# Reading the moving operand of a product column by column from its two halves in turn

## The chip, the cores and the metric

The kernel runs on one core of a Trainium2 chip. The metric is the device time of one execution in microseconds (us). Engines are named as the profile names them: PE is TensorE's matmul, PEld its weight load, DVE is VectorE, ACT is ScalarE, POOL is GpSimd, SP is SyncE, which here issues nearly all DMAs.

## The reference

Eight sequences of 3008 tokens with 256 channels go through a Fourier mixing layer, and all 24064 tokens then through a feed-forward layer of width 2048:

```python
def _attn_ref(x, w_r, w_i, b_r, b_i):
    X = np.fft.rfft(x, axis=1)
    Xr, Xi = (X.real.astype(np.float32), X.imag.astype(np.float32))
    Yr = Xr @ w_r - Xi @ w_i + b_r
    Yi = Xr @ w_i + Xi @ w_r + b_i
    lam = 0.01
    Yr = np.sign(Yr) * np.maximum(np.abs(Yr) - lam, 0.0)
    Yi = np.sign(Yi) * np.maximum(np.abs(Yi) - lam, 0.0)
    Y = Yr.astype(np.float64) + 1j * Yi.astype(np.float64)
    return np.fft.irfft(Y, n=x.shape[1], axis=1).astype(np.float32)

def _moe_ref(x, w_in, w_out):
    h = np.maximum(x @ w_in, 0.0)
    return (h * h @ w_out).astype(np.float32)
```

All of it is float32. Every token is a column of its own in the feed-forward layer: no step of that layer mixes two tokens.

## The kernel before

The Fourier transform of a sequence is cut into factors 47 and 64; its steps are small products on TensorE, with trips through DRAM scratch between them (steps a, b, mix, c and d in the names of tiles). The transform of the next sequences and the feed-forward layer of the present one run side by side.

The feed-forward layer works on chunks of `CH = 512` tokens, 47 of them (8 x 3008 / 512). A chunk's input stands in SBUF as `xt`, two tiles [128, 2, 512] of type float32r: the high part and the low part of the number, each with the 256 channels as two blocks of 128 partitions (index k) and the 512 tokens contiguous along the row. A float32 product is made of three products of such parts (`mm3`, lines 183 to 188: high times high, high times low, low times high).

The main loop (line 1115) runs over rounds; a round is one chunk and one of `NU = 8` pairs of hidden blocks, so there are 47 x 8 = 376 rounds. In a round:

- `mm1` (line 971), the first product, makes two blocks (a = 0, 1) of 128 hidden units by 512 tokens, `ph` in PSUM. The stationary operand is a 128x128 block of `w_in` (`wi`), the moving operand is `xt`, 512 columns wide. For each a there are two channel blocks k and three part products: 12 matmuls of 512 columns. In the rounds called `halved` (130 of them) the last product of the second block is cut into two of 256 columns (lines 983 to 986).
- `squares` (line 991) on ACT takes `ph` out of PSUM with Relu (line 995) and squares it (line 996) into `g`; `sums` on DVE makes three more combinations of quarter blocks, so that `g` has seven slabs of 256 columns. A slab combines the two hidden blocks and the two 256-column halves of the chunk.
- three rounds later (`LAG = 3`) `mm2` (line 1018), the second product, multiplies the seven slabs (split into `gh` and `gl`) by seven combinations of `w_out` blocks: 21 matmuls of 256 columns (14 at line 1023, 7 at line 1027), summed over the eight rounds of a chunk in four banks `po`. `put_together` then makes the 256 output channels by 512 tokens of the chunk and stores them contiguously in `outT`.

Between the two products a round may also hold the transform's matmuls: `psb` (line 228), `psd` (line 277), `psa`, `psm`, `psc` (through `mm3`). The order on each engine is written out by hand: `manual_schedule` keeps the order of the program text, and a plan of places (`p1`, `p2`, `e`, `f`, ...) puts the transform's steps into the rounds. On the host, `token_order()` puts the columns of `outT` back into the order of tokens.

## Time and profile before

| | |
|---|---|
| time, median of 3 runs | 2524.14 us (2523.18 to 2525.43) |
| span of the profiled execution, first to last instruction | 2521.5 us |
| median time less that span | 2.6 us |
| PE busy | 2503.5 us (99%) |
| PEld busy | 2260.2 us (90%) |
| DVE busy | 2097.8 us (83%) |
| ACT busy | 1991.8 us (79%) |
| POOL busy | 17.0 us (1%) |
| DMA engines, main queue | 20.9% of 16 engines |

The profiled execution has only its span listed, not a time of its own; the median of the timed runs stands 2.6 us above it. Busy time is the union of an engine's records. The duration of a matmul in a row runs from its start to a modelled end, and successive matmuls overlap in it; the pace of a stream of matmuls is read from the difference of their starts. A window is given in us from the start of the span.

### The profile page before, as it was taken

To read this page: it belongs to the slowest core of one execution; us is meant where nothing else is said; L and a number is where in the kernel's file an instruction comes from. 1 tells how busy PE (TensorE), PEld (TensorE's weight loads), DVE (VectorE), ACT (ScalarE), POOL (GpSimd) and SP (SyncE) were. 2 spreads that over 40 slices of the span, in tenths; PEclk is the share of its full clock that TensorE was granted. 3 is DMA by queue.
4 is the path that set the end of the run, shared out by engine and by line. 5 is a ranking of instruction groups with operands and counts; after the bars stand their busy time and mean duration, and the time that the engine had idled before them with its cause. 6 is when DMAs were issued, how large, how long until landed. Compare 5 with 4: busy or idle time off the path is not lost.

```text
span 2521.5 us, 42247 instructions
## 1 busy us (share of the span) xinstructions
PE 2503.5 (99%) x16648; PEld 2260.2 (90%) x16648; DVE 2097.8 (83%) x3179; ACT 1991.8 (79%) x2776; POOL 17.0 (1%) x29
## 2 busy tenths in 40 slices
PE   9999999999999999999999999999999999999999
PEld 5689999999999999999999999999999999999998
DVE  5798888888888888888888888888887888777776
ACT  4788887888788887888878878788787788777776
POOL 0100000000000000000000000000000000000000
PEclk9999999999999999999999999999999999999999
DMA  8612222222121121212122121221111111101000
GB/s 266 207 55 66 74 88 68 65 76 73 54 75 60 50 70 57 71 50 67 60 69 63 54 70 50 70 62 61 58 56 56 38 54 48 39 21 34 17 25 18
DMA packets 110622, 164.66 MB, mean 65 GB/s; under 512 B 9513, under 2 KB 59673, under 8 KB 110234
## 3 DMA queue, kind: packets, MB, share of 16 engines
q1 hardware_dynamic: 110282, 161.85, 20.9%
q8 instruction: 132, 2.16, 0.4%
q14 instruction: 64, 0.52, 0.1%
q10 hardware_dynamic: 144, 0.13, 0.0%
HBM read 86.97 MB, written 74.97 MB: 64 GB/s over the span
## 4 chain that ended last, share of the span: by engine, by line
PE 88%; ACT 5%; DVE 4%; issue 1%; DMA 1%; SPq 0%; DVEq 0%; ACTq 0%
PE po L1023 21%; PE ph L187 11%; PE ph L188 11%; PE ph L186 11%; PE po L1027 11%; PE psd L277 3%; PE psb L228 3%; PE psm L186 3%; PE psm L188 3%; PE psm L187 3%; ACT g L995 1%; PE ph L986 1%; PE ph L983 1%; PE ph L984 1%; ACT g L996 1%
## 5 line engine op out<-in xcount | busy, mean ns | idle before, releaser
L1137 DVE TENSOR_TENSOR gl<-g,gh 128x1792 fp32r<-128x1792 f32 x376 | 759.5, 2020 | 22.4 <-ACT gh L1132 15.4
L995 ACT ACTIVATE g<-ph 128x512 f32<-128x512 f32 x752 | 408.2, 595 | 417.1 <-PE ph L188 297.4
L1023 PE MATMUL po<-gh,wo 128*128 128x256 f32 x5250 | 681.5, 280 | 3.1 <-DVE o L1053 2.1
L1132 ACT CAST gh<-g 128x1792 fp32r<-128x1792 f32 x376 | 637.2, 1695 | 3.5 <-PE po L1023 0.8
L1023 PEld LDWEIGHTS po<-gh,wo 128*128 128x128 f32 x5250 | 631.2, 188 | 6.5 <-DVE o L1053 5.9
L186 PE MATMUL ph<-xt,wi 128*128 128x512 f32 x1374 | 538.2, 392 | 2.2 <-ACT g L995 2.0
L188 PE MATMUL ph<-xt,wi 128*128 128x512 f32 x1374 | 537.4, 391 | 0.0
L187 PE MATMUL ph<-xt,wi 128*128 128x512 f32 x1374 | 537.3, 391 | 0.0
L1001 DVE TENSOR_TENSOR g<-g 128x512 f32<-128x512 f32 x376 | 259.3, 690 | 290.3 <-ACT g L996 288.4
L996 ACT ACTIVATE g<-g 128x1024 f32<-128x1024 f32 x376 | 399.5, 1062 | 12.0
L1027 PE MATMUL po<-gl,wo 128*128 128x256 f32 x2625 | 359.2, 276 | 0.0
L1027 PEld LDWEIGHTS po<-gl,wo 128*128 128x128 f32 x2625 | 325.7, 188 | 0.0
L188 PEld LDWEIGHTS ph<-xt,wi 128*128 128x128 f32 x1374 | 258.0, 188 | 55.9
L186 PEld LDWEIGHTS ph<-xt,wi 128*128 128x128 f32 x1374 | 257.9, 188 | 49.6 <-ACT g L995 2.8
L187 PEld LDWEIGHTS ph<-xt,wi 128*128 128x128 f32 x1374 | 258.0, 188 | 44.3
L1003 DVE TENSOR_TENSOR g<-g 128x256 f32<-128x256 f32 x376 | 159.9, 425 | 12.9
L1002 DVE TENSOR_TENSOR g<-g 128x256 f32<-128x256 f32 x376 | 159.8, 425 | 12.9
L186 PE MATMUL psm<-wm,xh 128*128 128x256 f32 (+1 forms) x552 | 159.7, 289 | 1.6 <-ACT x L232 1.3
L188 PE MATMUL psm<-wm,xl 128*128 128x256 f32 (+1 forms) x552 | 158.2, 287 | 0.0
L187 PE MATMUL psm<-wm,xh 128*128 128x256 f32 (+1 forms) x552 | 158.0, 286 | 0.0
L277 PEld LDWEIGHTS psd<-tD,din 120*128 120x128 f32 (+1 forms) x832 | 108.2, 191 | 9.7 <-issue 1.9
L228 PEld LDWEIGHTS psb<-tB,bin 128*128 128x128 f32 x768 | 99.8, 191 | 13.1 <-issue 3.7
(139 smaller groups left out, 2800.5 us busy)
## 6 DMA issues: line engine op xcount, KB each, us to landing
bin<-s SPq DMA_DIRECT2D x96, 256.0 KB
s<-evc SPq DMA_DIRECT2D x96, 256.0 KB
outT_dram<-o SPq DMA_DIRECT2D x92, 256.0 KB
din<-s SPq DMA_DIRECT2D x96, 240.0 KB
xin<-in_xp_dram SPq DMA_DIRECT2D x72, 240.0 KB
s<-eva SPq DMA_DIRECT2D x72, 240.0 KB
s<-eva SPq DMA_DIRECT2D x38, 192.0 KB
w<-in_moe_w_in_dram SPq DMA_DIRECT2D x8, 512.0 KB
```

Source lines behind the costliest of these rows:

```text
L186: nc.tensor.matmul(out, l0, r0, start=start, stop=False, **kw)
L187: nc.tensor.matmul(out, l0, r1, start=False, stop=False, **kw)
L188: nc.tensor.matmul(out, l1, r0, start=False, stop=stop, **kw)
L228: nc.tensor.matmul(ps[:, k, :, q, :], tv[:, q, k], tB[:, 0:r + 2:r + 1], start=True, stop=True)
L277: nc.tensor.matmul(ps[:, k, part], t[:n, s:s + P], tD[:n, tab + part, :n], start=True, stop=True)
L995: nc.scalar.activation(g[:, 2 * a:2 * a + 2], ph[a].rearrange("p (t m) -> p t m", t=2), AF.Relu)
L996: nc.scalar.activation(g[:, 0:4], g[:, 0:4], AF.Square)
L1001: nc.vector.tensor_sub(g[:, 4:6], g[:, 1:4:2], g[:, 0:2])
L1023: nc.tensor.matmul(out, wo_[k][j][:, s], gh[:, s], start=j == 0 and half == 0 and k == 0, stop=False, skip_group_check=True)
L1027: nc.tensor.matmul(out, wo_[0][j][:, s], gl[:, s], start=False, stop=j == NU - 1, skip_group_check=True)
L1132: nc.scalar.copy(split_[r - 1][0], hid[r - 1])
L1137: nc.vector.tensor_sub(gl, hid.pop(r - 1), gh.bitcast(F32))
```

## The change

`crossed` is a view of a tile's row of 512 columns in which column 0 of the first half comes first, then column 0 of the second half, then column 1 of the first, column 1 of the second, and so on: an access pattern of 256 steps of 4 bytes with 2 steps of 1024 bytes inside it. `mm1` hands its moving operand to the matmuls in this view. The tiles themselves, what is written to them, the number of instructions and their order on every engine stay as they were; the rows of the instruction order differ by their line numbers alone. Column j of `ph`, and of all that follows, then belongs to another token of the same chunk, and numpy puts the columns of `outT` back after the run (`places`).

```diff
+def crossed(x):
+    return x.rearrange("p (a i) -> p i a", a=2)
+
+def places(n):
+    return np.arange(n).reshape(2, n // 2).T.reshape(-1)
...
-                w, x = (wi_[0][:, k, fs], wi_[1][:, k, fs]), (xts[c][0][:, k], xts[c][1][:, k])
+                w, x = (wi_[0][:, k, fs], wi_[1][:, k, fs]), (crossed(xts[c][0][:, k]), crossed(xts[c][1][:, k]))
                 if halved and a and k:
                     nc.tensor.matmul(ph[a], w[0], x[0], start=False, stop=False)
                     nc.tensor.matmul(ph[a], w[0], x[1], start=False, stop=False)
                     for n in range(0, CH, HALF):
-                        nc.tensor.matmul(ph[a][:, n:n + HALF], w[1], x[0][:, n:n + HALF], start=False, stop=n > 0)
+                        nc.tensor.matmul(ph[a][:, n:n + HALF], w[1], x[0][:, n // 2:(n + HALF) // 2], start=False, stop=n > 0)
                 else:
                     mm3(ph[a], w, x, k == 0, k == 1)
...
-    got = got.reshape(D, nb, S)
+    chunks = np.empty((D, nb * S // CH, CH), got.dtype)
+    chunks[:, :, places(CH)] = got.reshape(D, -1, CH)
+    got = chunks.reshape(D, nb, S)
```

## Rows read from the trace of the kernel before

**Rows 1.** The page: span, busy time (share) xinstructions, PE and its granted clock in tenths.

```profile
span 2521.5 us, 42247 instructions
PE 2503.5 (99%) x16648; PEld 2260.2 (90%) x16648; DVE 2097.8 (83%) x3179; ACT 1991.8 (79%) x2776; POOL 17.0 (1%) x29
...
PE   9999999999999999999999999999999999999999
...
PEclk9999999999999999999999999999999999999999
```

**Rows 2.** The page: chain of work that ended last, shares by engine and line.

```profile
PE 88%; ACT 5%; DVE 4%; issue 1%; DMA 1%; SPq 0%; DVEq 0%; ACTq 0%
PE po L1023 21%; PE ph L187 11%; PE ph L188 11%; PE ph L186 11%; PE po L1027 11%; PE psd L277 3%; PE psb L228 3%; PE psm L186 3%; PE psm L188 3%; PE psm L187 3%; ACT g L995 1%; PE ph L986 1%; PE ph L983 1%; PE ph L984 1%; ACT g L996 1%
```

**Rows 3.** Groups on PE: line, out<-in, shapes, xcount | busy us, mean ns | idle before.

```profile
L186 PE MATMUL ph<-xt,wi 128*128 128x512 f32 x1374 | 538.2, 392 | 2.2 <-ACT g L995 2.0
...
L187 PE MATMUL ph<-xt,wi 128*128 128x512 f32 x1374 | 537.3, 391 | 0.0
...
L986 PE MATMUL ph<-xt,wi 128*128 128x256 f32 x260 | 51.5, 280 | 0.0
L983 PE MATMUL ph<-xt,wi 128*128 128x512 f32 x130 | 50.6, 389 | 0.0
L984 PE MATMUL ph<-xt,wi 128*128 128x512 f32 x130 | 50.6, 389 | 0.0
```

**Rows 4.** Timeline of PE in one round: start us, us, engine line op.

```profile
1211.26 0.39 PE L186 MATMUL ph<-xt,wi 128*128 128x512 f32 x1
1211.49 0.40 PE L187 MATMUL ph<-xt,wi 128*128 128x512 f32 x1
...
1214.00 0.28 PE L186 MATMUL psa<-fh,tAs 120*120 120x256 f32 x1
...
1214.71 1.76 PE L1023 MATMUL po<-gh,wo 128*128 128x256 f32 x14
1216.31 0.96 PE L1027 MATMUL po<-gl,wo 128*128 128x256 f32 x7
1217.10 0.28 PE L186 MATMUL psm<-wm,xh 128*128 128x256 f32 x1
```

**Rows 5.** What PE waited for in the whole span: us in total, times, longest.

```profile
PE psa L488 <- DMA x<-in_xu_dram: 2.3, 2, 1.2
PE po L1023 <- DVE o L1053: 2.1, 11, 0.3
PE ph L186 <- ACT g L995: 2.0, 2, 1.6
```

**Rows 6.** Start-up: timeline of plain float32 matmuls, one line's durations (ns), window with PEclk.

```profile
21.63 6.17 PE L631 MATMUL idle<-x,tU 96*96 96x512 f32 x14
...
L631 PE MATMUL idle<-x,tU x28: 590/592/594, 21.6 to 115.5; 96*96 96x512 f32 x28
...
0.00:55.00 55.00, 50.48 (x173) 28.06 (x174) 28.30 (x50) 24.67 (x45) 4.34 (x8) 1.00 0.86 257
```

**Rows 7.** Groups on ACT and on DVE: xcount | busy us, mean ns | idle before.

```profile
L1132 ACT CAST gh<-g 128x1792 fp32r<-128x1792 f32 x376 | 637.2, 1695 | 3.5 <-PE po L1023 0.8
L996 ACT ACTIVATE g<-g 128x1024 f32<-128x1024 f32 x376 | 399.5, 1062 | 12.0
L995 ACT ACTIVATE g<-ph 128x512 f32<-128x512 f32 x752 | 408.2, 595 | 417.1 <-PE ph L188 297.4 <-PE ph L986 118.3
...
L1137 DVE TENSOR_TENSOR gl<-g,gh 128x1792 fp32r<-128x1792 f32 x376 | 759.5, 2020 | 22.4 <-ACT gh L1132 15.4
L1001 DVE TENSOR_TENSOR g<-g 128x512 f32<-128x512 f32 x376 | 259.3, 690 | 290.3 <-ACT g L996 288.4
```

**Rows 8.** Lines that read every second 4-byte word: min/median/max ns.

```profile
L306 DVE SCALAR_TENSOR_TENSOR w<-w,w x13: 691/693/827, 37.7 to 101.4; 128x512 uint32<-128x512 uint32 x13
...
L301 ACT ACTIVATE w<-w x13: 661/667/682, 35.0 to 96.6; 128x512 f32<-128x512 f32 x13
```

## The prediction

> **What bounds the kernel now.** I read the page's busy times first: PE is busy 2503.5 of 2521.5 us, in every slice, at a granted clock of nine tenths or more, while DVE has 83% and ACT 79% [rows 1]. Busy PE alone proves little, since a matmul's end is modelled; so next the chain of waits. It runs 88% through PE, and the three lines of the first product's helper (L186 to L188, tile ph) and the two of the second (L1023, L1027) make up most of it [rows 2]. Last, what PE waited for: the longest three entries are 2.3, 2.1 and 2.0 us in the whole span [rows 5]. So the kernel is a stream of matmuls on PE with nearly nothing between them. All that PE idles is 2521.5 less 2503.5, 18.0 us. A time added to each matmul of the first product therefore goes into the end one for one, except for at most those 18 us; a time added to ACT or DVE would not.

> **The change, part by part.**

> *Instructions.* None is added, removed or moved; only the read pattern of the first product's moving operand differs. Weight loads, PSUM addresses, semaphores and all work of ACT, DVE and SP stay. These cost nothing, and no cover is needed for that. The host's reordering lies outside the device time.

> *How many matmuls are touched.* Lines 186, 187 and 188 have 1374 matmuls of 512 columns each on ph (the row of 188 repeats the other two), lines 983 and 984 have 130 each, and line 986 has 260 of 256, worth 130 of 512 [rows 3]. 3 x 1374 + 2 x 130 + 130 = 4512 matmuls of 512 columns, which is 376 rounds x 12.

> *What one costs today.* The rows' mean of 391 ns contains an overlapping end, so I take starts: the round that begins at 1211.26 has its twelve until 1214.00, where the next product starts [rows 4]: 2.74 us / 12 = 228 ns. For comparison the 14 matmuls of 256 columns from 1214.71 to 1216.31 take 114 ns each, and the 7 up to 1217.10 take 113 [rows 4]. Half the columns, half the time: a matmul is paid by the column, 0.446 ns each, with next to no fixed part. That is 2.25 columns, each of 4 bytes per partition, per ns. 4512 x 228 ns = 1029 us, 41% of the span, is what the change can act on.

> *What one will cost.* No row of before reads a moving operand in which every next word lies far from the last. I bound it. From below: the array still takes one column at a time, and if the reader fetches any column at 0.446 ns, the price is 0. A gain I exclude, because nothing is taken away and the same columns stream. From above I look for the rate at which things in this trace take one 4-byte word per step. ACT goes from 1062 to 1695 ns between 1024 and 1792 elements a row [rows 7]: 633 / 768 = 0.824 ns an element. DVE goes from 690 to 2020 ns between 512 and 1792 [rows 7]: 1.04 ns. And TensorE itself, with plain float32 instead of float32r, at a granted clock of 1.00: fourteen matmul records of 512 columns take 6.17 us, the last of them 0.592 [rows 6], so (6.17 - 0.592) / 13 = 429 ns each, or 0.838 ns a column. So of the readers in the trace the float32r stream alone exceeds about 1.2 words per ns, and it does so by a factor of nearly two. The plain reading of that is that it gets two neighbouring words from one step of its reader. The new pattern leaves no two neighbours together: words alternate between places 1024 bytes apart. Then each step yields one column, and the pace falls to that of one word per step.

> I take the row on the same engine, 429 ns: 429 - 228 = +201 ns a matmul, x 4512 = +907 us. With ACT's pace it would be 0.824 x 512 = 422 ns, +194, +875 us; with a doubling of today's pace 456 ns, +228, +1029 us.

> *What hides it.* Nothing beyond the 18 us of idle time. PEld is independent and short: a longer stream gives weight loads more cover. ACT waits for ph already (417 us of idle before L995 [rows 7]), so it follows PE; the squares, slabs and splits of a round keep their duration in a longer round. The second product's operands come three rounds earlier, so they are ready. **The sum:** the median 2524.1 lies 2.6 us above the profiled span, and I add the difference to the median: 2524 + 907 = 3431 us. Its own range: from 2524 + 875 - 18 = 3381 up to 2524 + 1029 = 3553.

> [...]

> **The rivals.**

> *The reader doesn't care: not slower.* Mechanism: the address of every column is generated singly, at the rate of the array, and each partition's memory gives any word at that rate. It holds as long as the reader serves 2.25 scattered words per ns; then the price is 0 and the time stays at 2524. For it: DVE reading every second 4-byte word (L306, 692 ns for 512) is no slower than DVE reading all of them (L1001, 690), and ACT (L301, 667 ns) is near the 640 ns that 1062 - 512 x 0.824 gives for a dense row [rows 7, 8]. Against: that gap is one word, not 1020 bytes, and those engines ask for half as many words per ns. So these rows say little on the step that decides, and I give it 0.28, of which 0.01 falls on a small gain. That the new pattern is merged back into one run is no likely way to this result, since 4-byte steps with 1024-byte steps inside them cannot be one run.

> *Part of the price.* The reader keeps two fetched pieces, one of each half, and serves some columns from them: somewhere between. With half of the 201 ns the time is 2524 + 453 = 2977. Against it: the trace shows no reader at a pace between 0.45 and 0.82 ns a word. 0.07.

> *More than one step a column.* Each word pays its own latency: at DVE's 1.04 ns, 512 x 1.04 = 532 ns, +304, x 4512 = +1372, 3896 us; at two of ACT's steps, 844 ns, +616, 5303 us. [...] 0.10 together.

> **How the numbers follow.** The likely case has what is left: 0.55, at 3431 us. A difference within 0.2% (5 us) is about what a measurement of this kernel cannot tell from no change. Faster 0.01, the same 0.27, slower 0.55 + 0.07 + 0.10 = 0.72. The cases have two heaps far apart. To leave out no more than 2 in 10 the range must reach down to the unchanged time, and up to a full doubling: 2519 to 3560, which leaves out the 0.10 above, part of the 0.01 and the rim of the likely case. The likely case's own range is 3380 to 3560.

> **What would show it.** Right: the groups on ph rise in mean from 391 to about 590 ns, as in L631's rows, and the starts within a round are some 430 ns apart, while psa, po and psm keep 114 to 120 ns and the granted clock stays 1.00; DVE and ACT keep their busy us but fall to about 61% and 58% of the span; the idle time before L995 grows by hundreds of us, still with ph as releaser. Wrong: starts on ph still 228 ns apart (the reader doesn't care), or well over 460 (more than a step a column). If the ph groups lengthen but the end moves less than 4512 times that, then my claim that nothing hides them is wrong. [...]

## The result

The changed kernel takes 2488.8 us (median of 4 runs, 2485.9 to 2491.6) where the kernel before takes 2523.7 us beside it: the ratio is 0.9862, with a 95% interval of 0.9848 to 0.9876. It is 35 us faster, 1.4%. I had forecast 3431 us, and a range of 2519 to 3560.

The page of the changed kernel: its span, its busy times, PE with its granted clock, and the chain of waits. All lines named here stand ten numbers higher than before.

```profile
span 2484.1 us, 42247 instructions
PE 2462.0 (99%) x16648; PEld 2272.8 (91%) x16648; DVE 2095.0 (84%) x3179; ACT 1990.9 (80%) x2776; POOL 17.1 (1%) x29
...
PEclk9999999999999999999999999999999999999999
...
PE 82%; DVE 8%; ACT 7%; issue 2%; DMA 1%; SPq 0%; DVEq 0%; ACTq 0%
```

PE is still busy all the time and at the same granted clock (1.00 over the span, before and now); its busy time fell by 41.5 us [rows 1]. DVE and ACT do the same work. The chain now leaves PE for DVE and ACT more often, 15% of it against 9% [rows 2].

The groups on PE, as in [rows 3], with the second product's two lines: line, out<-in, shapes, count, busy us, mean ns, idle before.

```profile
L1033 PE MATMUL po<-gh,wo 128*128 128x256 f32 x5250 | 687.3, 282 | 5.1 <-DVE o L1063 4.2 <-DVE o L1046 0.6 <-ACT xt L299 0.2
L196 PE MATMUL ph<-xt,wi 128*128 128x512 f32 x1374 | 523.1, 381 | 3.5 <-ACT g L1005 3.4
L198 PE MATMUL ph<-xt,wi 128*128 128x512 f32 x1374 | 520.8, 379 | 0.0
L197 PE MATMUL ph<-xt,wi 128*128 128x512 f32 x1374 | 520.7, 379 | 0.0
L1037 PE MATMUL po<-gl,wo 128*128 128x256 f32 x2625 | 360.9, 277 | 0.0
...
L996 PE MATMUL ph<-xt,wi 128*128 128x256 f32 x260 | 49.9, 274 | 0.0
L993 PE MATMUL ph<-xt,wi 128*128 128x512 f32 x130 | 49.3, 379 | 0.0
L994 PE MATMUL ph<-xt,wi 128*128 128x512 f32 x130 | 49.3, 379 | 0.0
```

The first product's matmuls fell from 391 to 379 ns. Its six groups, which were 538.2 + 537.4 + 537.3 + 51.5 + 50.6 + 50.6 = 1765.6 us, are now 1713.1: 52.5 us gained. The timeline of a round, to be held against [rows 4], shows the pace:

```profile
1196.00 0.38 PE L196 MATMUL ph<-xt,wi 128*128 128x512 f32 x1
1196.22 0.38 PE L197 MATMUL ph<-xt,wi 128*128 128x512 f32 x1
...
1198.59 0.29 PE L196 MATMUL psa<-fh,tAs 120*120 120x256 f32 x1
...
1199.31 1.76 PE L1033 MATMUL po<-gh,wo 128*128 128x256 f32 x14
1200.91 0.96 PE L1037 MATMUL po<-gl,wo 128*128 128x256 f32 x7
1201.70 0.28 PE L196 MATMUL psm<-wm,xh 128*128 128x256 f32 x1
```

Twelve matmuls from 1196.00 to 1198.59 are 216 ns each, where there were 228; the other products keep their 113 to 120 ns. In the whole trace the median distance of two starts on ph is 216 ns against 227 before. The two crossed matmuls of 256 columns in a halved round start 109 ns apart, so that 256 columns more cost 107 ns: 2.39 columns per ns. At that rate 512 columns take 214 ns, an estimate from these two distances (2 x 107): the dense read was 6% above it, and the crossed read is 1% above it. I call it the array's own pace; that the array and not the reader sets it is not shown.

Of the 52.5 us the profiled span keeps 37.4 (the medians of the timed runs lie 35 apart). The rest of PE's busy time grew by 11.0 us, most of it at L1033 (681.5 to 687.3), and PE's idle time grew from 18.0 to 22.1 us. What PE waited for, beside [rows 5]:

```profile
PE po L1033 <- DVE o L1063: 4.2, 16, 0.3
PE ph L196 <- ACT g L1005: 3.4, 4, 1.7
PE psm L196 <- ACT x L242: 1.5, 1, 1.5
```

So the kernel gained where I had forecast a loss, on the very instructions that I had named. The question for the experiments was what the reader of the moving operand does.

### The profile page after: what moved, and what is told of

The parts are those of the page before. It is cut to its first block, busy times and chain, and to the rows that moved or that the text cites. A ratio compares the mean times of both kernels' runs of the same rounds, so it can differ in the third digit from the quotient of the medians.

```text
span 2484.1 us, 42247 instructions
## 1 busy us (share of the span) xinstructions
PE 2462.0 (99%) x16648; PEld 2272.8 (91%) x16648; DVE 2095.0 (84%) x3179; ACT 1990.9 (80%) x2776; POOL 17.1 (1%) x29
## 4 chain that ended last, share of the span: by engine, by line
PE 82%; DVE 8%; ACT 7%; issue 2%; DMA 1%; SPq 0%; DVEq 0%; ACTq 0%
PE po L1033 20%; PE po L1037 10%; PE ph L196 10%; PE ph L198 10%; PE ph L197 10%; PE psd L287 3%; PE psb L238 3%; PE psm L196 3%; PE psm L198 3%; PE psm L197 2%; DVE gl L1147 2%; ACT g L1005 2%; ACT g L1006 1%; DVE g L1011 1%; ACT gh L1142 1%
## 5 line engine op out<-in xcount | busy, mean ns | idle before, releaser
L1147 DVE TENSOR_TENSOR gl<-g,gh 128x1792 fp32r<-128x1792 f32 x376 | 759.5, 2020 | 22.4 <-ACT gh L1142 16.2
L1033 PE MATMUL po<-gh,wo 128*128 128x256 f32 x5250 | 687.3, 282 | 5.1 <-DVE o L1063 4.2
L1033 PEld LDWEIGHTS po<-gh,wo 128*128 128x128 f32 x5250 | 635.4, 189 | 9.3 <-DVE o L1063 7.4
L196 PE MATMUL ph<-xt,wi 128*128 128x512 f32 x1374 | 523.1, 381 | 3.5 <-ACT g L1005 3.4
L198 PE MATMUL ph<-xt,wi 128*128 128x512 f32 x1374 | 520.8, 379 | 0.0
L197 PE MATMUL ph<-xt,wi 128*128 128x512 f32 x1374 | 520.7, 379 | 0.0
L1006 ACT ACTIVATE g<-g 128x1024 f32<-128x1024 f32 x376 | 399.2, 1062 | 12.0
```

Of the source, the lines that this page charges most:

```text
L196: nc.tensor.matmul(out, l0, r0, start=start, stop=False, **kw)
L197: nc.tensor.matmul(out, l0, r1, start=False, stop=False, **kw)
L198: nc.tensor.matmul(out, l1, r0, start=False, stop=stop, **kw)
L1006: nc.scalar.activation(g[:, 0:4], g[:, 0:4], AF.Square)
L1033: nc.tensor.matmul(out, wo_[k][j][:, s], gh[:, s], start=j == 0 and half == 0 and k == 0, stop=False, skip_group_check=True)
L1147: nc.vector.tensor_sub(gl, hid.pop(r - 1), gh.bitcast(F32))
```

## Twelve orders in one kernel

From here on "pace" is the median distance of the starts of two successive matmuls of equal width on the same tile (512 columns where nothing else is said), over all the rounds of a kind. It is taken from the start times in the trace. The mean durations in the rows are some 160 to 200 ns above it, because they hold a modelled end.

```diff
+ORDERS = (("A", "p n -> p n", {}),
+          ("B", "p (a i) -> p i a", dict(a=2)),
+          ("C", "p (a i u) -> p i a u", dict(a=2, u=2)),
... D, E, F: the same with u=4, 16, 64
+          ("G", "p (b a u) -> p b u a", dict(a=2, u=4)),
... H: the same with u=16
+          ("I", "p (i a) -> p a i", dict(a=2)),
... J, K: the same with a=4, 16
+          ("L", "p (a i) -> p i a", dict(a=4)))
...
-                w, x = (wi_[0][:, k, fs], wi_[1][:, k, fs]), (xts[c][0][:, k], xts[c][1][:, k])
+                w, x = (wi_[0][:, k, fs], wi_[1][:, k, fs]), (viewed(xts[c][0][:, k], c), viewed(xts[c][1][:, k], c))
```

The edit is made on the kernel before; `viewed` rearranges by the order of the chunk.

> Chunk c reads the first product's moving operand in one of twelve orders of its 512 columns (c modulo 12; tile names phA to phL): A as stored; halves in turn in runs of 1 (B, the change), 2 (C), 4 (D), 16 (E) and 64 columns (F); neighbouring blocks of 4 (G) or 16 columns (H) in turn, column by column; sweeps with a step of 2 (I), 4 (J) and 16 columns (K); four quarters in turn (L). In the two traces so far a matmul of 512 columns starts 227 ns after the one before it when read as stored and 216 ns when crossed. Theory 1 (a dense run of words in one piece of memory makes the reader stumble now and then, any order that leaves the piece at each word is free of it): A 227; B, J, K and L 216; C and I, where two words of a piece of 16 bytes still follow each other, between; D, E and F 227; G and H 216. Theory 2 (the moving operand and the next weight load walk through memory in step and meet in the same bank; only an order far from a plain walk avoids it): A, E, F near 227, G, H and I, which stay near the plain walk, near 227 too, B, K and L 216. Theory 3 (the values that follow each other on the array set the pace, through its power): the pace follows how alike neighbouring tokens are, nearly every order has its own, D to F between A and B. My rule of before, one word per step, would have G to L at 420 or more; it has fallen with the result.

Groups of this kernel on PE, one line of `mm3` for each order:

```profile
L226 PE MATMUL phA<-xt,wi 128*128 128x512 f32 x115 | 45.0, 391 | 0.0
L225 PE MATMUL phG<-xt,wi 128*128 128x512 f32 x118 | 44.7, 379 | 0.0
L225 PE MATMUL phH<-xt,wi 128*128 128x512 f32 x117 | 44.3, 379 | 0.0
L226 PE MATMUL phI<-xt,wi 128*128 128x512 f32 x120 | 75.9, 633 | 0.0
L226 PE MATMUL phJ<-xt,wi 128*128 128x512 f32 x113 | 72.5, 642 | 0.0
L226 PE MATMUL phK<-xt,wi 128*128 128x512 f32 x111 | 67.8, 611 | 0.0
L226 PE MATMUL phC<-xt,wi 128*128 128x512 f32 x124 | 62.9, 507 | 0.0
L226 PE MATMUL phD<-xt,wi 128*128 128x512 f32 x114 | 47.5, 417 | 0.0
L226 PE MATMUL phL<-xt,wi 128*128 128x512 f32 x90 | 39.7, 441 | 0.0
```

All three theories of the expectation miss much of it. Theory 1 had the sweeps J and K at 216, and they have 461 and 433; theory 2 had G and H at 227, and they have 216. What I had called fallen, one word per step, stands there too: the sweeps I, J and K go at about half the dense pace (452, 461 and 433 ns), near the 429 ns that I forecast, whatever their step. And yet orders that alternate between two places, next to each other (G) or 1024 bytes apart (B), are faster than the dense walk.

Theory 4, formed on these rows: the columns are read as if by **two streams, one for the even and one for the odd places of the order**. Each keeps the piece of four columns (16 bytes) that it read last, and pieces arrive at one per about 0.85 ns for both together (K's 433 ns / 512). That a piece has four columns is read from the rows: G, with blocks of four, gains all that B gains (216 ns both), and in I, where the columns of each stream lie four apart, every column costs a piece (452 ns, near J's 461 and K's 433). A dense walk then takes two columns per stream from each piece, 256 pieces or some 217 ns for 512 columns, with no slack against the 214 ns that I estimate for the array. Alternating halves take four, and there is slack. A sweep takes one, 512 pieces, twice the dense time. That having no slack is what costs the dense walk its 11 ns is my reading; the count by itself gives it 217 ns.

## Weights or values?

```diff
+SHIFT = dict(G=4, H=8, I=16, J=32)
...
+    s = min(f * P + SHIFT.get(kind, 0), DFF - P)
+    if kind in "BF":
...
+        w = w[:, s:s + 2 * P:2]
+    elif kind == "C":
+        w = w[:, f::NF]
+    else:
+        w = w[:, s:s + P]
+    if kind == "F":
+        x = crossed(x)
+    if kind == "D":
+        x = x[:, 0:1].broadcast_to([P, CH])
+    if kind == "E":
+        w = w[:, 0:1].broadcast_to([P, P])
...
-                if halved and a and k:
+                if False:
```

`NF` is 16. The last two lines leave out the cut of a matmul in the halved rounds, so that this kernel has 130 matmuls fewer.

> Leaves the right result: in chunks of nine of ten kinds the first product takes wrong weights or one repeated column (c modulo 10; tile names phA to phJ); only its pace is read. The moving operand is read as stored except in D (one column 512 times) and F (crossed). The weights are read as stored in A and D, with a step of 2 columns in B and F, a step of 16 columns in C, one column 128 times in E, and from a start that is 4, 8, 16 or 32 columns further in G to J. Theory 1 (the dense run of the moving operand itself stumbles): A, B, C, E and G to J all 227, F 216, D may be either. Theory 2 (weight load and moving operand meet in a bank): B, C or E moves away from 227, to 216 where the weight load stays out of the way (E above all), and G to J differ among each other; F need not be 216. Theory 3 (values): D and E, where nothing changes from column to column or from weight to weight, 216; G to J 227.

```profile
L221 PE MATMUL phA<-xt,wi 128*128 128x512 f32 x160 | 62.5, 391 | 0.0
L221 PE MATMUL phB<-xt,wi 128*128 128x512 f32 x160 | 63.0, 394 | 0.0
L221 PE MATMUL phC<-xt,wi 128*128 128x512 f32 x160 | 63.7, 398 | 0.0
L221 PE MATMUL phD<-xt,wi 128*128 128x512 f32 x160 | 60.6, 379 | 0.0
L221 PE MATMUL phE<-xt,wi 128*128 128x512 f32 x160 | 63.3, 396 | 0.0
L221 PE MATMUL phF<-xt,wi 128*128 128x512 f32 x160 | 60.6, 379 | 0.0
L221 PE MATMUL phG<-xt,wi 128*128 128x512 f32 x160 | 63.2, 395 | 0.0
```

No way of reading the weights frees the dense read of its surplus: B, C and E, the weight load that stays on one column, have 233, 236 and 233 ns. Theory 2 had one of them fall to 216, and F perhaps not at 216; so the place of the weights does not make the surplus. What the weight load as such adds to it stays open, because no run leaves it out. And the dense read does depend on the weights a little, as theory 2 had it for G to J: its pace is 227 ns from the old start and 231 to 233 ns from each of the four others. The crossed read (F) and the read of one repeated column (D) stay at 216. Of theory 3, E at 233 says that equal weights give nothing; D fits it as well as theory 4, and the next run tells them apart.

```diff
-        nc.scalar.copy(xt_of(c)[0][:, :, at:at + n], xf[:, :, of:of + n])
+        for o in range(2):
+            t = at + o
+            d, m = t % 2 * HALF + t // 2, (n - o + 1) // 2
+            if m:
+                nc.scalar.copy(xt_of(c)[0][:, :, d:d + m], xf[:, :, of + o:of + n:2])
... the low part on DVE in the same way; crossed(...) in mm1 stays for even chunks only
```

This edit is made on the changed kernel.

> The high and low parts of the chunk are stored with even tokens in the first half of the row and odd tokens in the second (ACT and DVE write each piece in two instructions). Even chunks (phP) read the halves in turn, so that the array gets the tokens in their old order from crossed addresses; odd chunks (phQ) read the row as stored, so that it gets them in another order from dense addresses. Theories 1 and 2 (addresses): phP 216 ns from start to start, phQ 227. Theory 3 (values): phP 227, phQ another pace.

```profile
L203 PE MATMUL phP<-xt,wi 128*128 128x512 f32 x702 | 266.1, 379 | 0.0
L203 PE MATMUL phQ<-xt,wi 128*128 128x512 f32 x672 | 262.8, 391 | 0.0
```

Old order of values from crossed addresses (phP): 216 ns. New order of values from dense addresses (phQ): 227. The addresses decide, not the values; theory 3 fell. With half of the chunks crossed the kernel took 2510.3 us in its one run.

## Ten more orders, chosen against theory 4

```diff
+ORDERS = (("A", "p n -> p n", {}),
+          ("M", "p (a i r) -> p r i a", dict(a=2, r=2)),
... N: the same with r=4
+          ("P", "p (b a u) -> p b u a", dict(a=4, u=4)),
... Q, R, S: the same with a=2, u=2; a=2, u=8; a=8, u=8
+          ("W", "p (a i u) -> p i a u", dict(a=4, u=2)),
+          ("X", "p (a i) -> p i a", dict(a=8)),
+          ("Y", "p (a i u) -> p i a u", dict(a=4, u=4)))
```

> As in the kernel with twelve orders, now ten others by chunk (phA, phM, phN, phP to phS, phW to phY). Theory 4, formed on those twelve: columns are read by two streams, one for the even and one for the odd places of the order; each keeps the 16-byte piece (four columns) it read last, and all pieces come at one per 0.83 ns. Dense: each stream takes 2 columns from a piece, 256 pieces, 213 ns, just at the array's pace, so it stumbles (227). Halves in turn: 4 from a piece, 128 pieces, slack (216). A sweep with a step takes 1, 512 pieces, 427 ns or more. Theory 5: a pair as innermost loop is read in one step, wherever its two columns lie. A as stored: 227 by both. M, halves in turn with a step of 2 (0, 256, 2, 258): theory 4 has 2 a piece, 227 to 254; theory 5 has 216. N, halves in turn with a step of 4: theory 4 has 1 a piece, 427 to 460; theory 5 has 216. Q (0, 2, 1, 3): theory 4 has 2 a piece, 227; theory 5 has 216. R (0, 8, 1, 9): 216 by both. W (runs of 2 from four quarters): theory 4 has 512 pieces, up to 430, at least the 333 of the runs of 2 from halves. Y (runs of 4 from four quarters): 250 to 260 as from halves. P (0, 4, 8, 12, 1), S (eight blocks of 8 in turn) and X (eight strips of 64 in turn): a stream goes between 2, 4 and 4 pieces and comes back to them; 430 if it keeps but one, 216 if it keeps all; the quarters in turn gave 275, so I expect 275 for P and more for S and X.

```profile
L223 PE MATMUL phM<-xt,wi 128*128 128x512 f32 x148 | 57.9, 391 | 0.0
L223 PE MATMUL phQ<-xt,wi 128*128 128x512 f32 x146 | 57.1, 391 | 0.0
L223 PE MATMUL phR<-xt,wi 128*128 128x512 f32 x141 | 53.4, 379 | 0.0
L223 PE MATMUL phN<-xt,wi 128*128 128x512 f32 x148 | 93.7, 633 | 0.0
L223 PE MATMUL phW<-xt,wi 128*128 128x512 f32 x121 | 76.5, 632 | 0.0
L223 PE MATMUL phS<-xt,wi 128*128 128x512 f32 x145 | 88.4, 610 | 0.0
L223 PE MATMUL phP<-xt,wi 128*128 128x512 f32 x147 | 63.6, 433 | 0.0
L223 PE MATMUL phY<-xt,wi 128*128 128x512 f32 x115 | 50.0, 435 | 0.0
```

M, N, Q and R came as theory 4 had them, and S and X above P. Its numbers missed Y (266 ns, forecast 250 to 260) and W (443, forecast 430 at most), and P came a little low (268 for 275).

Both kernels with many orders in one table; the pieces are theory 4's count for 512 columns.

| columns a stream takes from a piece before it leaves it | pieces | orders (first columns) and pace in ns |
|---|---|---|
| 4 | 128 | B (0 256 1 257) 216; G (0 4 1 5) 216; R (0 8 1 9) 216; H (0 16 1 17) 216 |
| 2 | 256 | A (0 1 2 3) 227; M (0 256 2 258) 227; Q (0 2 1 3) 227 |
| 1 | 512 | I (0 2 4 6) 452; J (0 4 8) 461; K (0 16 32) 433; N (0 256 4 260) 452 |
| 2, with jumps of 1024 or 512 bytes between runs | 256 | F (runs of 64) 227; E (16) 240; D (4) 254; Y (4, from quarters) 266 |
| 1, coming back to one of 2 pieces | 512 | L (0 128 256 384) 275; P (0 4 8 12) 268; C (0 1 256 257) 333 |
| 1, coming back to one of 4 pieces | 512 | W (0 1 128 129) 443; S (0 8 16 24) 432; X (0 64 128 192) 487 |

The first three lines are as theory 4 has them, eleven orders in three groups. Theory 5, an inner pair read in one step, fell with M, Q and N. One memory of recent pieces shared by all columns is excluded too: by it A, Q, B, G and R would all need 128 pieces and M 256, but B, G and R have 216 and A, Q and M have 227. The last three lines show where the theory is too simple: jumps between dense runs cost up to 39 ns more at the same 256 pieces, the more the shorter the runs; with two pieces to return to, a stream pays more than if it kept both and less than if it kept one; with four it keeps none. I have no rule for that. As wholes the two kernels took 2835.0 and 2948.9 us in one run each. No order here tells whether the pieces of the two streams come in turn, one per 0.85 ns, or two at once, one pair per 1.7 ns: in all of them both streams change their piece at the same pair of places.

## The orders as whole kernels

```diff
+ORDERS = (("K", "p (i a) -> p a i", dict(a=16)),)
... the second kernel:
+ORDERS = (("M", "p (a i r) -> p r i a", dict(a=2, r=2)),)
... the third:
+ORDERS = (("G", "p (b a u) -> p b u a", dict(a=2, u=4)),)
```

The rest of each edit is that of the kernels with many orders, made on the kernel before.

> All chunks read the first product's moving operand as a sweep with a step of 16 columns (0, 16, 32, ..., then 1, 17, ...), the order K that took 433 ns by chunk. This is the step of my prediction by itself: if one word per step goes into the end one for one, as I summed it, the time is 2524 + 4512 x (433 - 228) = 2524 + 925 = 3449 us, and ACT and DVE keep their busy us. If the longer rounds give something back (waits that vanish, the 18 us of idle time), 3420 to 3440; if the granted clock falls, far above.

3444.1 us in one run, against 3449 by the sum. The busy times on its page:

```profile
PE 3431.3 (100%) x16648; PEld 2369.5 (69%) x16648; DVE 2111.4 (61%) x3179; ACT 1997.4 (58%) x2776; POOL 17.0 (0%) x29
```

And the first of its groups on PE:

```profile
L214 PE MATMUL ph<-xt,wi 128*128 128x512 f32 x1374 | 840.0, 611 | 0.0
```

A price per matmul does go into the end nearly one for one, PE's idle time falls from 18 to 11 us (3442.3 us of span), and DVE and ACT are at the 61% and 58% that I had worked out.

> All chunks read the halves in turn, but in each half first the even columns, then the odd ones (0, 256, 2, 258, ...; order M). Theory 4: each of the two streams takes 2 columns from a piece of four, as in the dense order; no gain: ph at 227 to 229, ratio to before 0.997 to 1.004. Theory 5 (what helps is only that the two halves are in turn): the gain of the change, 0.986.

Ratio 1.0002, interval 0.9993 to 1.0011, with ph back at 227: halves in turn, but two columns of a piece for each stream, and the whole gain is gone.

> All chunks read neighbouring blocks of four columns in turn (0, 4, 1, 5, 2, 6, 3, 7, then the next eight; order G). Theory 4: each stream takes 4 columns from a piece, as with the change: ph at 216, ratio 0.985 to 0.988. If it were the distance of 1024 bytes between the two columns that helped: no gain, 0.997 to 1.003.

Ratio 0.9853, interval 0.9837 to 0.9870, with ph at 216: neighbouring blocks of 16 bytes do what halves 1024 bytes apart do. The distance has no part in what is gained.

## Where the gain can be had again

```diff
-                nc.tensor.matmul(out, wo_[k][j][:, s], gh[:, s], start=j == 0 and half == 0 and k == 0,
+                nc.tensor.matmul(out, wo_[k][j][:, s], crossed(gh[:, s]), start=j == 0 and half == 0 and k == 0,
...
-            nc.tensor.matmul(out, wo_[0][j][:, s], gl[:, s], start=False, stop=j == NU - 1,
+            nc.tensor.matmul(out, wo_[0][j][:, s], crossed(gl[:, s]), start=False, stop=j == NU - 1,
```

First this is done on the changed kernel.

> The change in the second product too: its moving operands gh and gl are read with the two halves of each 256-column slab in turn. If what is gained belongs to any dense float32r moving operand (theory 1), its 7896 matmuls of 256 columns fall from 113 to 114 ns each to about 109, 4.5 ns x 7896 = 35 us, less what waits for ACT and DVE take back: 2455 to 2475 us, ratio to before 0.973 to 0.981. If it belongs to the meeting of xt and wi alone (theory 2 with other places for gh and wo), the second product keeps its pace or changes it either way: 2480 to 2495 us, ratio 0.983 to 0.989.

Ratio 0.9788, interval 0.9775 to 0.9801: 2470.8 us, 18.0 us below the change. The second product in its rows:

```profile
L1033 PE MATMUL po<-gh,wo 128*128 128x256 f32 x5250 | 667.4, 278 | 6.4 <-DVE o L1063 4.8 <-DVE o L1046 0.8 <-ACT xt L299 0.5
L1037 PE MATMUL po<-gl,wo 128*128 128x256 f32 x2625 | 354.4, 275 | 0.0
```

Its pace fell from 113 to 114 ns to 112, not to 109 as in the halved matmuls of the first product (109 ns crossed, 113 dense). psd and psb, which have 120 and 128 columns, go at 111 to 112 ns as well; a pace that does not depend on the columns fits the weight load, which each of these matmuls has. In the last kernel of this section psa, with 256 crossed columns and weights of 120 columns instead of 128, comes down to 109, which fits too. I take the weight load for what holds po now; no run took it away.

The same edit on the kernel before, so that the first product stays dense:

> The crossed order in the second product alone (gh and gl), the first reads as stored. With both, the second product's matmuls started 111.7 ns apart on the mean, against 115.0 with the change alone, and the time was 18.0 us below that of the change. If the two gains do not hang on each other, this kernel is 18 to 22 us below before: 2502 to 2506 us, ratio 0.991 to 0.993, with po at 112 ns and ph at 227 to 229. If the second product's gain came from the shorter rounds of the first, or the other way round, po stays at 114 and the time within 0.3% of before.

Missed: 2515.9 us, ratio 0.9973 (0.9962 to 0.9983), 7.5 us where I had expected 18 to 22.

```profile
L1033 PE MATMUL po<-gh,wo 128*128 128x256 f32 x5250 | 666.1, 278 | 4.5 <-DVE o L1063 4.1 <-DVE o L1046 0.4
L198 PE MATMUL ph<-xt,wi 128*128 128x512 f32 x1374 | 541.5, 394 | 0.0
...
L196 PE MATMUL psm<-wm,xh 128*128 128x256 f32 (+1 forms) x552 | 161.5, 293 | 0.2
```

The second product gained all of its 20 us (681.5 + 359.2 before, 666.1 + 354.4 now), but the dense reads beside it slowed down: ph by 7 us, psm by 5. In the changed kernel po had slowed down in the same way, and it no longer does once it is crossed too. So the two gains are not additive: 35 and 7.5 us each alone, 53 together.

The starts in the traces show where this time goes: a dense stream starts slowly and then settles. In the kernel before, the first three distances between a round's matmuls on ph have medians of 232, 233 and 231 ns, and from the fourth on 227; in the changed kernel they are 215 or 216 from the first on. With the second product alone crossed, more of the round passes before ph settles: 49% of the distances are 229 ns or more, against 32% before. The dense po in most rounds settles at 113 to 114 ns; its last three distances are still 116 or more in 67 of 373 rounds of the changed kernel, and in 10 before. Why a dense stream settles sooner or later, or not at all, is not shown.

```diff
+                    (crossed(s["h"][:, cs]), crossed(s["l"][:, cs])), True, True)
... psa above, psm below (one of two places); the host stores their columns in the order of places(256)
+                        (crossed(wm[0][:, mat, k]), crossed(wm[1][:, mat, k])), k == 0, k == 1)
... psc and ACT's copy of it
+                tuple(s[k].rearrange("p q e -> p e q") for k in ("zh", "zl")), True, True)
+            nc.scalar.copy(e.rearrange("p (q e) -> p q e", q=2), s["ps"].rearrange("p (e q) -> p q e", q=2))
```

This comes on top of both products.

> Crossed orders wherever a float32r moving operand is read: both products, the mixing (psm), the folded transform (psa), where the host stores the columns so that the crossed read gives them in their old order, and the way back (psc), whose two halves are told apart again by ACT as it copies PSUM out. By theory 4 a 512-column matmul goes to 216 ns wherever it has 234 to 237 (psc: 252 x 20 ns = 5 us), and the 256-column ones to 109 to 112 (psm: 1656 x 2.5 ns = 4 us; psa: 468 x 8 ns = 4 us): 13 us below the kernel with both products, 2458 us, ratio 0.974. If the remaining time waits for ACT and DVE or for weight loads, less: 2462 to 2470. ACT's copy of psc may take longer than its 0.585 us, as it reads PSUM at every second word.

Ratio 0.9755, interval 0.9742 to 0.9769: 2461.4 us, 62 us below the kernel before and the fastest of all. The way back and ACT's copy of it:

```profile
L197 PE MATMUL psc<-zl,tMs 128*128 128x512 f32 x84 | 31.8, 379 | 0.0
...
L870 ACT COPY evc<-psc 128x512 f32<-128x512 f32 x84 | 49.5, 589 | 0.0
```

Against the kernel with both products psc goes from 234 to 218 ns, psa from 118 to 109, psm from 114 to 112. ACT reads every second word of PSUM at 589 ns, against 584 in a row. Of the 13 us that I had summed 9.4 came.

## Why the prediction was wrong, point by point

**What bounds the kernel:** right. PE is the bound, and a price per matmul reaches the end; the sweep kernel gave 3444 where the same sum with its own pace says 3449. A gain reaches it less fully: of 52.5 us on ph 37.4 came, and the slower dense matmuls of the other products took 11.0 and idle time 4.1.

**Instructions and count:** right. Nothing else moved, 4512 matmuls are touched, nothing hides them.

**What one costs today:** read and not asked. "a matmul is paid by the column, 0.446 ns each" took 228 ns for the price of 512 columns on the array. The crossed read showed 216, and the array's own pace is 214 by the estimate above: 12 to 14 ns a matmul were a surplus of reading, and 12 of them are the gain. Proportion to the columns (228 and 114 ns) did not show that it was the array's price, since the surplus is in both.

**"A gain I exclude, because nothing is taken away":** wrong, by the step before. A stream that runs 6% above the array's estimated pace can gain without any work being taken away. I gave that outcome a chance of 0.01 and no case of its own.

**What one will cost:** the step that failed, and with it the term of +201 ns a matmul. The forecast rests on "it gets two neighbouring words from one step of its reader" and "The new pattern leaves no two neighbours together". What the runs showed in its place is -12 ns (216 against 228). A pace near the one that I took from ACT and from plain float32 is there: K goes at 433 ns, and the forecast had 429. That the three have one cause is not shown, and the nearness may be luck: a plain float32 product makes two records of its 512 columns (L615 issues 2 and has 4), so its 429 ns need not be a rate of reading at all. But by the orders measured the reader behaves as if it were two streams, and the pattern's inner pair puts one half of the row on each; within its stream each column's neighbour follows at once. What counts is the columns that a stream takes from a piece (B and G 216 ns, M and Q 227), not whether neighbours arrive together. I costed a sweep; the change is two dense walks. I also misread a row: DVE's 1.04 ns an element at L1137 is for two operands, g and gh [rows 7], so some 1.9 words per ns, and the float32r stream was not the only reader above 1.2.

**The rivals:** "the reader doesn't care" was nearest in time and wrong in kind: it cares by a factor of two (216 ns for the change, 433 to 461 for the sweeps). Its rows on ACT and DVE said nothing on the matter, as I had noted. The others fell; the granted clock was 0.999 or 1.000 in every profiled execution and not under 0.998 in any other.

**The range** reached to the unchanged time and no further down. Its lower end should have been the array's own pace, by the estimate above: 4512 x (228 - 214) = 63 us below, of which the crossed read reached 4512 x (228 - 216) = 54 on ph.

## What to carry to other kernels

Where a float32r moving operand is read densely, hold the distance of the starts, at a granted clock of 1.00, against 0.42 ns a column, which is what the last 256 of 512 crossed columns cost here (107 ns), before calling the stream bound by the array. If it is some per cent above and the order of the columns is free, try reading two places in turn, so that even and odd places of the order each walk through neighbouring words: in this kernel that was worth 5% of every 512-column matmul, and 2.5% of the time when done in nearly every product. A sweep of the moving operand with a step of two columns already halved the pace here (452 ns against 227); a step between columns that follow each other cost nothing only where two walks in turn left each stream at least two columns of a piece one after the other (M and Q, 227 ns), and gained only where they left it four (B, G, H and R, 216 ns).
